# A planner that knows traced durations and the SBUF ports that VectorE and GpSimd share, in an attention-and-FFN kernel on one core

## Chip, core and metric

The kernel runs on one core of a Trainium2 chip. The metric is device time in microseconds: before, 1008.44 us is the median of three runs (1007.25 to 1010.76). One execution was profiled: its own time is 1007.83 us, and its span, from the first to the last instruction, is 1005.8 us. Engines carry the names of the profile: PE is TensorE (PEld its weight loads), DVE is VectorE, ACT is ScalarE, POOL is GpSimd, SP is SyncE, which issues the DMAs.

## The reference

Thresholded attention for 8 batches, 8 heads, 576 positions and head dimension 64, then a gated FFN over all heads side by side (512 columns), all in float32:

```python
scores = q @ k.T / sqrt(64)
scores = where(scores >= max(scores) - tau, scores, -1e9)
attn = exp(scores - max(scores))
attn = attn / (sum(attn) + 1e-9)
x = attn @ v                                  # heads side by side: 8 x 576 x 512
x_prev = x shifted by one position, zero first
xk = mu_k * x + (1 - mu_k) * x_prev
xr = mu_r * x + (1 - mu_r) * x_prev
out = sigmoid(xr @ w_r) * (relu(xk @ w_k) ** 2 @ w_v)
```

## The kernel before

**Attention.** The work is cut into 32 jobs (8 batches by 4 pairs of heads). `operands` loads q and k of a job (`rq`, `rk`) and splits them into high and low parts for TensorE (`qa`, `qb`, `kc`): copies on ACT (L480, L498), one subtraction on POOL (L488), one on DVE (L508). A job has five units: four blocks of 128 queries for both heads, and "T", the last 64 queries of both heads together. For a unit `scores` runs the matmuls (L578, for T L562) into PSUM tiles `s` (three buffers, which the outputs of attention use too). `softmax` then takes for each of the nine score tiles of a job the negated row maximum on DVE (L624), adds the threshold to it (L632), runs a steep Prelu and an Exp with row sum on ACT (L640, L648); `invert` adds 1e-9 to the row sums and takes the reciprocal on DVE (L656, L657), for both heads of a unit in one instruction each; POOL scales the rows (L671); `turn` transposes 32x32 blocks on DVE (L688, L692). `attend` multiplies by v on PE (L717), and ACT puts the result into `xT` (L743; two buffers, one per batch in flight) and `xE` (L750). The row statistics of a unit lie in a tile `sm` of 128 x 4 x 2: the statistic first, then the head.

**Weights.** w_k, w_r and w_v come in as 64-bit words in 20 pieces of 512 KB. `weight` rebuilds each piece and splits it: ACT L397, DVE L405, L419, L426, L436, ACT L443, POOL L447, in four scratch columns inside `xT[1]`.

**FFN.** 18 chunks of 256 positions: two "main" ones per batch and one "end" chunk for the last 64 positions of four batches. `ffn_chunk` mixes x and its shifted copy (POOL L816, DVE L825), splits the mix (ACT L838, POOL L846), multiplies by w_k (PE L868), squares and splits (ACT L876 to L881, POOL L891), multiplies by w_r (L910) and w_v (L932), applies the sigmoid (ACT L918) and the gate (DVE L938).

**Order.** No engine's order is written by hand. Each step is added to a `Plan` with its engine, `occ` (how long it holds the engine), `lat` (when its result is there; `occ + 0.1` if not given), a key, and the tiles it reads and writes. `Plan.order` is a list scheduler: it goes through time with its own model of the engines, at each turn takes for each engine the step that could start first (ties by key) and of these the earliest one. The key is the place in the program plus a number for the step's kind (`NUDGE`; `FIRST` for the first 60 keys); `AHEAD` moves attention's PE steps ahead of the FFN's, `LATE` adds to their dependences after time `FROM`. W0 to W3 are the times from which the planner lets the loads of the 20 pieces start. What comes out is only the order of each engine's instructions; on the chip they run when what they wait for is there.

```python
                    t = max(t, f)
                    late = t + s.soft
                    ...
                    k = (late, s.key, i, t)
                    if pick is None or k < pick:
                        pick = k
                if pick is not None and (best is None or pick[0] < best[0]):
                    best = (pick[0], e, pick[2], pick[3])
```

Of the kernel before, what the change touches and what calls it, by code (L numbers as in the profile page):

```python
# [7 lines left out]
F32 = mybir.dt.float32  # L8
FR = mybir.dt.float32r
AF = mybir.ActivationFunctionType  # L10
ALU = mybir.AluOpType
# [38 lines left out]
class Plan:  # L50
# [3 lines left out]
    HOP, LATE, FROM, AHEAD = 0.05, 0.05, 200.0, 65.0  # L54
    SOFT = {"DVE": 0, "ACT": 0}
    NUDGE = {
# [7 lines left out]
    }  # L64
    FIRST, UNTIL = {
# [8 lines left out]
    CHUNK, FETCH = 256, 3.55  # L74
# [62 lines left out]
    def order(self, loose=()):  # L137
# [904 lines left out]
```

## Time and profile before

| | |
|---|---|
| median of three runs | 1008.44 us |
| profiled execution, its own time | 1007.83 us |
| its span | 1005.8 us |
| PE busy | 900.2 us, 90% of the span |
| ACT busy | 794.9 us, 79% |
| DVE busy | 705.8 us, 70% |
| POOL busy | 588.6 us, 59% |
| mean granted TensorE clock | 0.948 of full |

Busy shares are means over stages that differ, so the span is read in stages below. A matmul's time in the profile overlaps that of the next one; what a piece of PE work really takes is read from the distance between starts. An idle engine costs time only where its work is what ends last.

### The profile page before, as it was taken

Reading aid. Unit: us, or ns where it says so; the run is one execution under the profiler, and the core shown is the slowest. Engines: PE = TensorE matmul, PEld = TensorE weight load, DVE = VectorE, ACT = ScalarE, POOL = GpSimd, SP = SyncE. Lnnn points to the kernel's source line nnn. Section 1 sums busy time; section 2 is a strip of 40 time slices with the busy share of each in tenths; the row PEclk is TensorE's granted clock in tenths of the full one; section 3 lists DMA queues with packets and bytes.
Section 4 is the critical chain, followed back from the end, with each engine's and each line's share of the span. In section 5 each row is a group of like instructions: output and inputs, shape, how many; then the busy total and the mean of one; then the engine's idle time right before and its main releaser. Section 6 shows DMA issues by size and latency. Waiting matters only on the chain.

```text
span 1005.8 us, 32052 instructions
## 1 busy us (share of the span) xinstructions
PE 900.2 (90%) x13520; PEld 790.3 (79%) x13520; DVE 705.8 (70%) x1434; ACT 794.9 (79%) x1660; POOL 588.6 (59%) x576
## 2 busy tenths in 40 slices
PE   3355669899989999999999999999999999999988
PEld 3244558798878988898889798888888888889876
DVE  5979999677878686868686958686858677741130
ACT  5766878788889898989898798888898979854422
POOL 1756667665656665756565657565666657543431
PEclk9577778899999999999999999999999999999999
DMA  7562231233323232333222223332322222210001
GB/s 282 179 252 82 89 105 50 72 117 103 110 96 117 96 117 96 117 97 103 98 99 91 77 76 117 96 117 84 118 72 89 94 90 73 70 49 22 22 22 22
DMA packets 31599, 97.48 MB, mean 97 GB/s; under 512 B 3808, under 2 KB 3808, under 8 KB 27360
## 3 DMA queue, kind: packets, MB, share of 16 engines
q1 hardware_dynamic: 31456, 95.44, 28.1%
q8 instruction: 106, 1.74, 0.7%
q14 instruction: 37, 0.30, 0.1%
HBM read 85.99 MB, written 9.44 MB: 95 GB/s over the span
## 4 chain that ended last, share of the span: by engine, by line
PE 43%; DVE 9%; ACT 4%; POOL 3%; issue 2%; ACTq 0%; DVEq 0%; POOLq 0%
PE w L868 13%; PE s L717 8%; PE w L932 7%; PE w L910 7%; PE s L578 6%; DVE r L825 3%; DVE sm L624 2%; DVE sq L688 2%; PE s L562 2%; POOL sq L671 1%; POOL xk L846 1%; ACT sq L640 1%; ACT sq L648 1%; ACT L648 1%; DVE sm L656 1%
## 5 line engine op out<-in xcount | busy, mean ns | idle before, releaser
L671 POOL TENSOR_SCALAR sq<-sq,sm 128x576 f32<-128x576 f32 x288 | 239.4, 843 | 162.4 <-DVE sm L657 90.6
L624 DVE TENSOR_REDUCE sm<-s 128x1 f32<-128x576 f32 x288 | 211.9, 745 | 81.6 <-PE s L578 75.7
L640 ACT ACTIVATE sq<-s,sm 128x576 f32<-128x576 f32 x288 | 206.4, 737 | 59.2 <-DVE sm L632 55.5
L868 PE MATMUL w<-xk,wk 128*128 128x256 f32 x1728 | 228.8, 285 | 4.0 <-ACT xk L838 2.3
L868 PEld LDWEIGHTS w<-xk,wk 128*128 128x128 f32 x1728 | 217.7, 191 | 9.6 <-issue 4.2
L648 ACT ACTIVATE sq<-sq,small 128x576 f32<-128x576 f32 x288 | 222.9, 777 | 2.0
L932 PE MATMUL w<-wv,k 128*128 128x512 f32 x864 | 215.2, 394 | 0.0
L688 DVE STREAM_TRANSPOSE sq<-sq 128x1152 f32<-128x1152 f32 x128 | 175.5, 1371 | 54.8 <-POOL sq L671 54.5
L717 PE MATMUL s<-sq,v 32*64 32x144 f32 x9216 | 177.8, 292 | 19.2 <-issue 8.4
L717 PEld LDWEIGHTS s<-sq,v 32*64 32x64 f32 x9216 | 151.0, 133 | 44.2 <-issue 23.8
L932 PEld LDWEIGHTS w<-wv,k 128*128 128x128 f32 x864 | 157.8, 188 | 32.5 <-issue 3.6
L578 PE MATMUL s<-kc,qa 128*128 128x288 f32 x512 | 128.4, 334 | 50.3 <-ACT sq L640 37.6
L578 PEld LDWEIGHTS s<-kc,qa 128*128 128x128 f32 x512 | 88.7, 204 | 78.0 <-ACT sq L640 35.2
L488 POOL TENSOR_TENSOR kc<-rk,kc 64x576 fp32r<-64x576 f32 x64 | 96.8, 1517 | 82.0 <-issue 60.8
L846 POOL TENSOR_TENSOR xk<-r,xk 128x512 fp32r<-128x512 f32 x72 | 95.3, 1324 | 83.8 <-ACT xk L838 82.8
L578 PE MATMUL s<-kc,qb 128*128 128x288 f32 x512 | 117.7, 314 | 0.0
L891 POOL TENSOR_TENSOR k<-r,k 128x512 fp32r<-128x512 f32 x72 | 93.2, 1298 | 40.1 <-ACT k L881 38.1
L910 PE MATMUL w<-wr,xk 128*128 128x512 f32 x432 | 107.1, 393 | 0.0
L825 DVE SCALAR_TENSOR_TENSOR r<-r,mu_sb,xT 128x256 f32<-128x256 f32 x128 | 73.9, 618 | 37.9 <-POOL xk L846 22.3
L578 PEld LDWEIGHTS s<-kc,qb 128*128 128x128 f32 x512 | 89.5, 205 | 1.2 <-issue 1.2
L910 PEld LDWEIGHTS w<-wr,xk 128*128 128x128 f32 x432 | 78.9, 189 | 14.5 <-ACT r L876 0.3
L838 ACT ACTIVATE xk<-r 128x512 fp32r<-128x512 f32 x72 | 45.2, 628 | 54.6 <-DVE r L825 54.3
(53 smaller groups left out, 915.2 us busy)
## 6 DMA issues: line engine op xcount, KB each, us to landing
v<-in_v SPq DMA_DIRECT2D x32, 1152.0 KB, 5.1
rq<-in_qk SPq DMA_DIRECT2D x64, 288.0 KB, 2.9
rk<-in_qk SPq DMA_DIRECT2D x64, 288.0 KB, 2.9
out<-sg SPq DMA_DIRECT2D x32, 256.0 KB, 2.1
wk<-in_w_k SPq DMA_DIRECT2D x8, 512.0 KB, 7.9
wv<-in_w_v SPq DMA_DIRECT2D x8, 512.0 KB, 10.5
wr<-in_w_r SPq DMA_DIRECT2D x4, 512.0 KB, 6.5
out<-sg SPq DMA_DIRECT2D x8, 128.0 KB, 2.4
```

Source lines behind the costliest of these rows:

```text
L578: PE.matmul(ss[y].get()[:, z, 0:HS], l.get()[:, c * P : (c + 1) * P], r.get()[:, keys(z)], start=(j == 0), stop=(j == 1),)
L624: lambda sv=sv, col=col: V.tensor_reduce(col(0), sv(), axis=AX.XY, op=ALU.max, negate=True),
L640: lambda st=st, pv=pv, col=col: A.activation(pv(), st(), AF.Prelu, bias=col(1), alpha=STEEP),
L648: lambda y=y, col=col: A.activation(part(y), part(y), AF.Exp, bias=small.get()[:, 3:4], accum_out=col(2)),
L671: lambda y=y: G.tensor_scalar(part(y), part(y), sm.get()[:, 3, y : y + 1], 0.0, op0=ALU.mult, op1=ALU.add),
L688: V.transpose(t, t)
L717: PE.matmul(os[a // 2].get()[hs, a % 2, 0:NX], vt.get()[rows, j, hs], sq.get()[rows, j, h], start=(j == 0), stop=(j == NB - 1),)
L825: V.scalar_tensor_tensor(d.get()[:, y, o : o + n], diff.get()[:, y, o : o + n], mu_sb.get()[:, j, hc + y : hc + y + 1], prv[:, hc + y], op ...
L846: lambda j=j, d=d, cs=cs: G.tensor_tensor(mix[j].get()[:, 1, cs], d.get(), mix[j].get()[:, 0, cs].bitcast(F32), op=ALU.subtract),
L868: PE.matmul(h.get()[:, f], l, r, start=(ct == 0 and i == 0), stop=(ct == NCT - 1 and i == 2))
L910: PE.matmul(z.get(), l, r, start=(ct == 0 and i == 0), stop=(ct == NCT - 1 and i == 2))
L932: PE.matmul(vps.get(), l, r, start=(ft == 0 and i == 0), stop=(ft == NFT - 1 and i == 2))
```

## The change

The planner is told other numbers and one more rule; the arithmetic of the kernel stays. First, `occ` and `lat` of most steps are set to durations from a trace. Second, steps on POOL and the DVE kinds in `PORT` (the four weight steps L405 to L436, L508 and L825) exclude each other in the planner's time: none of the one side starts before the last one of the other has ended. Third, the keys, `AHEAD`, `LATE` and the times of the weight loads have other values. Fourth, the tile `sm` is now 128 x 2 x 4, so that the two heads' sums of a unit lie four columns apart instead of side by side. Lines of the changed kernel stand 7 lower than before (L578 is now L585, L868 now L875).

```diff
-    HOP, LATE, FROM, AHEAD = 0.05, 0.05, 200.0, 65.0
+    HOP, LATE, FROM, AHEAD = 0.05, 0.3, 200.0, 120.0
     NUDGE = {
-        "act1": -59.5, "act10": 67.0, "act11": -222.0, "act12": -115.0, "act13": 59.5, "act14": -52.5, "act15": 165.0,
+        "act1": -99.5, "act10": 60.5, "act11": -242.0, "act12": -214.0, "act13": 90.5, "act14": -122.0, "act15": 167.5,
...
+    PORT = {"dve5", "dve6", "dve7", "dve8", "dve7b", "dve14"}
...
+        port = {}
...
                     t = max(t, f)
+                    if e == "POOL" or s.kind in self.PORT:
+                        t = max(t, port.get("DVE" if e == "POOL" else "POOL", 0.0))
                     late = t + s.soft
...
             s.start = t
+            if e == "POOL" or s.kind in self.PORT:
+                port[e] = t + s.occ
...
-    W0, W1, W2, W3, AVK = 3.220, 2.801, 34.671, 0.000, 1.0
+    W0, W1, W2, W3, AVK = 2.696, 1.270, 14.345, 0.000, 1.0
...
             "DVE",
-            0.65,
+            0.6,
             lambda: V.scalar_tensor_tensor(
                 u(), word(0), 29, u(), op0=ALU.logical_shift_right, op1=ALU.bitwise_or
             ),
             reads=[words],
             writes=box,
-            key=key, kind="dve8",
+            key=key, lat=0.68, kind="dve8",
...
-        sm = unit["sm"] = sbuf("sm", [P, 4, 2], F32, 4)
+        sm = unit["sm"] = sbuf("sm", [P, 2, 4], F32, 4)
...
-                return sm.get()[:, j, y : y + 1]
+                return sm.get()[:, y, j : j + 1]
...
-            V.tensor_scalar(sm.get()[:, 2, ysl], sm.get()[:, 2, ysl], 1e-9, None, op0=ALU.add)
-            V.reciprocal(sm.get()[:, 3, ysl], sm.get()[:, 2, ysl])
+            V.tensor_scalar(sm.get()[:, ysl, 2], sm.get()[:, ysl, 2], 1e-9, None, op0=ALU.add)
+            V.reciprocal(sm.get()[:, ysl, 3], sm.get()[:, ysl, 2])
```

What moves is seen at three places. The first is SP's queue from the start of the program: v and the first pieces of the weights, then q and k of jobs 1 and 2. Before, the queue stands so from its 14th DMA on:

```order
L471 DMA rk_136<-in_qk 128x576
L388 DMA wk_0_145<-in_w_k 128x512
L388 DMA wk_0_173<-in_w_k 128x512
L388 DMA wk_0_196<-in_w_k 128x512
L463 DMA rq_219<-in_qk 128x576
L388 DMA wk_0_224<-in_w_k 128x512
L463 DMA rq_229<-in_qk 128x576
L388 DMA wk_0_243<-in_w_k 128x512
L471 DMA rk_250<-in_qk 128x576
L471 DMA rk_287<-in_qk 128x576
L463 DMA rq_323<-in_qk 128x576
L388 DMA wr_0_331<-in_w_r 128x512
```

Now from its 14th:

```order
L478 DMA rk_123<-in_qk 128x576
L470 DMA rq_131<-in_qk 128x576
L395 DMA wk_0_140<-in_w_k 128x512
L470 DMA rq_145<-in_qk 128x576
L395 DMA wk_0_147<-in_w_k 128x512
L395 DMA wk_0_157<-in_w_k 128x512
L395 DMA wr_0_187<-in_w_r 128x512
L395 DMA wr_0_192<-in_w_r 128x512
L395 DMA wr_0_202<-in_w_r 128x512
L395 DMA wr_0_207<-in_w_r 128x512
L395 DMA wv_0_214<-in_w_v 128x512
L395 DMA wv_0_221<-in_w_v 128x512
```

All 20 pieces now stand ahead of the first load for job 2; before, the four loads of q and k for job 2 and one for job 3 stood ahead of the last twelve pieces.

The second place is DVE up to the first transpose of job 0 (L688 and L692, now L695 and L699). Before:

```order
L405 TENSOR_SCALAR xT_72<-xT_72 128x512
L632 TENSOR_SCALAR sm_177<-sm_177,small 128x1
L419 TENSOR_SCALAR xT_72<-xT_72 128x512
L656 TENSOR_SCALAR sm_147<-sm_147 128x1
L657 RECIPROCAL sm_147<-sm_147 128x1
L624 TENSOR_REDUCE sm_177<-s_183 128x1
L426 SCALAR_TENSOR_TENSOR xT_72<-wk_0_86,xT_72 128x512
L632 TENSOR_SCALAR sm_177<-sm_177,small 128x1
L692 STREAM_TRANSPOSE sq_149<-sq_149 128x36x16
```

Now:

```order
L433 SCALAR_TENSOR_TENSOR xT_72<-wk_0_116,xT_72 128x512
L412 TENSOR_SCALAR xT_72<-xT_72 128x512
L443 SCALAR_TENSOR_TENSOR xT_72<-wk_0_116,xT_72 128x512
L515 SCALAR_TENSOR_TENSOR qb_305<-rq_145,small,qa_301 128x576
L426 TENSOR_SCALAR xT_72<-xT_72 128x512
L433 SCALAR_TENSOR_TENSOR xT_72<-wk_0_140,xT_72 128x512
L443 SCALAR_TENSOR_TENSOR xT_72<-wk_0_140,xT_72 128x512
L412 TENSOR_SCALAR xT_72<-xT_72 128x512
L426 TENSOR_SCALAR xT_72<-xT_72 128x512
L695 STREAM_TRANSPOSE sq_152<-sq_152 128x36x32
```

Before, the first piece was still unfinished at that transpose; now six are finished there.

The third place is PE around the first matmul of the FFN (L868, now L875), with score matmuls (L578, now L585) and the T units (L562, now L569) beside it. Before:

```order
L578 MATMUL s_1632<-kc_1290,qb_1294 128x288 x2
L868 MATMUL w_1649<-xk_1120,wk_0_246 128x256 x3
L868 MATMUL w_1649<-xk_1120,wk_0_281 128x256 x3
L578 MATMUL s_1662<-kc_1585,qa_1575 128x288 x2
L578 MATMUL s_1662<-kc_1585,qb_1589 128x288 x2
L578 MATMUL s_1670<-kc_1290,qa_1280 128x288 x2
L578 MATMUL s_1670<-kc_1290,qb_1294 128x288 x2
L868 MATMUL w_1649<-xk_1120,wk_0_298 128x256 x3
```

Now:

```order
L585 MATMUL s_1661<-kc_1297,qa_1289 128x288 x2
L585 MATMUL s_1661<-kc_1297,qb_1337 128x288 x2
L569 MATMUL s_1678<-kc_1297,bd 128x288 x4
L569 MATMUL s_1678<-kc_1579,bd 128x288 x4
L875 MATMUL w_1694<-xk_1213,wk_0_209 128x256 x3
L875 MATMUL w_1694<-xk_1213,wk_0_256 128x256 x3
L585 MATMUL s_1707<-kc_1579,qa_1576 128x288 x2
L585 MATMUL s_1707<-kc_1579,qb_1636 128x288 x2
```

The T unit of the sixth job has moved ahead of the first FFN matmul; before it came 16 rows behind it. On PE the last 75 rows are the same in both, save for line numbers.

## Rows read from the trace of the kernel before

**Rows 1.** The page: span, engines, and 40 slices of 25.1 us.

```profile
span 1005.8 us, 32052 instructions
...
PE 900.2 (90%) x13520; PEld 790.3 (79%) x13520; DVE 705.8 (70%) x1434; ACT 794.9 (79%) x1660; POOL 588.6 (59%) x576
...
PEclk9577778899999999999999999999999999999999
```

**Rows 2.** Windows: start:end, length, busy us (instructions) by engine, PE clock, DMA.

```profile
0.00:12.50 12.50, 2.25 (x9) 2.25 (x10) 2.56 (x8) 4.69 (x9) 2.98 (x6) 1.00 0.78 280
12.50:152.60 140.10, 74.99 (x1357) 62.25 (x1356) 130.95 (x244) 105.67 (x227) 80.42 (x74) 0.71 0.43 153
152.60:210.00 57.40, 53.83 (x812) 47.32 (x812) 45.46 (x92) 46.16 (x99) 39.42 (x36) 0.91 0.22 78
210.00:905.20 695.20, 677.14 (x10815) 597.02 (x10813) 509.13 (x1040) 602.35 (x1270) 431.36 (x428) 1.00 0.29 95
905.20:1005.80 100.60, 92.04 (x539) 81.44 (x531) 17.66 (x52) 36.06 (x59) 34.43 (x34) 0.97 0.07 22
```

**Rows 3.** Waits on PE, 210 to 910 us: total, times, longest.

```profile
PE s L578 <- ACT sq L640: 5.1, 9, 0.9
PE s L717 <- ACT sq L640: 4.5, 4, 2.2
```

**Rows 4.** Groups of DVE instructions by form, 12.5 to 152.6 us: busy, mean ns.

```profile
L624 DVE TENSOR_REDUCE sm<-s 128x1 f32<-128x576 f32 x47 | 34.5, 744 | 10.9 <-PE s L578 10.0 <-PE s L562 0.9
...
L405 DVE TENSOR_SCALAR xT<-xT 128x512 f32<-128x512 f32 x17 | 11.9, 720 | 0.0
L508 DVE SCALAR_TENSOR_TENSOR qb<-rq,small,qa 128x576 fp32r<-128x576 f32 x11 | 11.7, 1073 | 0.0
L419 DVE TENSOR_SCALAR xT<-xT 128x512 uint32<-128x512 uint32 x17 | 10.7, 644 | 0.0
...
L825 DVE SCALAR_TENSOR_TENSOR r<-r,mu_sb,xT 128x256 f32<-128x256 f32 x6 | 5.7, 984 | 0.0
L656 DVE TENSOR_SCALAR sm<-sm 128x2 f32<-128x2 f32 x18 | 4.8, 269 | 0.2 <-ACT sq L648 0.2
...
L656 DVE TENSOR_SCALAR sm<-sm 128x1 f32<-128x1 f32 x5 | 0.7, 143 | 0.0
```

**Rows 5.** Single lines, whole span: count, shortest/median/longest in ns.

```profile
L405 DVE TENSOR_SCALAR xT<-xT x20: 402/419/1644, 18.5 to 175.9; 128x512 f32<-128x512 f32 x20
...
L419 DVE TENSOR_SCALAR xT<-xT x20: 409/423/1493, 18.9 to 177.3; 128x512 uint32<-128x512 uint32 x20
...
L508 DVE SCALAR_TENSOR_TENSOR qb<-rq,small,qa x64: 770/810/2035, 6.9 to 861.7; 128x576 fp32r<-128x576 f32 x64
...
L825 DVE SCALAR_TENSOR_TENSOR r<-r,mu_sb,xT x128: 443/479/1660, 94.6 to 941.4; 128x256 f32<-128x256 f32 x128
```

**Rows 6.** Timeline of DVE, then of POOL, from 618 us: start, length.

```profile
618.81 1.26 DVE L656 TENSOR_SCALAR sm<-sm 128x2 f32<-128x2 f32 x1
...
618.14 1.91 POOL L846 TENSOR_TENSOR xk<-r,xk 128x512 fp32r<-128x512 f32 x1
```

**Rows 7.** Timeline of PE, DVE and SP's queue in the first stage.

```profile
59.98 0.46 PE L717 MATMUL s<-sq,v 32*64 32x144 f32 x4 [3.93 <-issue]
...
61.21 0.76 DVE L624 TENSOR_REDUCE sm<-s 128x1 f32<-128x576 f32 x1 [4.97 <-PE s L578]
...
43.90 7.64 SPq L388 DMA_DIRECT2D wv<-in_w_v  x8
```

**Rows 8.** Timeline of PE late in the long stretch.

```profile
863.99 0.42 PE L578 MATMUL s<-kc,qa 128*128 128x288 f32 x2
...
865.05 1.55 PE L932 MATMUL w<-wv,k 128*128 128x512 f32 x6
...
875.99 0.53 PE L578 MATMUL s<-kc,qa 128*128 128x288 f32 x2
876.36 0.43 PE L578 MATMUL s<-kc,qb 128*128 128x288 f32 x2
```

More of the change, by code (lines that the diff above doesn't have):

```diff
@@ L399, in weight @@
             writes=box,
-            key=key, kind="act1",
+            key=key, lat=0.67, kind="act1",
         )
@@ L403, in weight @@
             "DVE",
-            0.4,
+            0.333,
             lambda: V.tensor_scalar(t(), t(), W_MIN, W_MAX, op0=ALU.max, op1=ALU.min),
             writes=box,
-            key=key, kind="dve5",
+            key=key, lat=0.42, kind="dve5",
         )
@@ L430, in weight @@
             writes=box,
-            key=key, kind="dve7",
+            key=key, lat=0.69, kind="dve7",
         )
@@ L440, in weight @@
             writes=box,
-            key=key, kind="dve8",
+            key=key, lat=0.68, kind="dve8",
         )
-        add("ACT", 0.53, lambda: A.activation(piece.get()[:, 0], t(), AF.Copy), reads=box, writes=[(piece, 0)], key=key, kind="act2")
+        add("ACT", 0.52, lambda: A.activation(piece.get()[:, 0], t(), AF.Copy), reads=box, writes=[(piece, 0)], key=key, lat=0.63, kind="act2")
         add(
             "POOL",
-            1.27,
+            1.24,
             lambda: G.tensor_tensor(piece.get()[:, 1], t(), piece.get()[:, 0].bitcast(F32), op=ALU.subtract),
@@ L449, in weight @@
             writes=[(piece, 1)],
-            key=key, kind="pool1",
+            key=key, lat=1.28, kind="pool1",
         )
@@ L482, in operands @@
                 writes=[both],
-                key=key - PREP, kind="act4",
+                key=key - PREP, lat=0.68, kind="act4",
             )
@@ L492, in operands @@
                 writes=[both],
-                key=key - PREP, kind="pool2",
+                key=key - PREP, lat=1.44, kind="pool2",
             )
@@ L502, in operands @@
                 writes=[top],
-                key=key - PREP, kind="act3",
+                key=key - PREP, lat=0.78, kind="act3",
             )
@@ L517, in operands @@
                 writes=[low],
-                key=key - PREP, kind="dve7b",
+                key=key - PREP, lat=0.81, kind="dve7b",
             )
@@ L553, in scores @@
                         writes=[(bd, (v_, h))],
-                        key=key - 3, kind="act5",
+                        key=key - 3, lat=0.25, kind="act5",
                     )
@@ L626, in softmax @@
                 writes=[(sm, (0, y))],
-                key=key - KMAX, kind="dve9",
+                key=key - KMAX, lat=0.75, kind="dve9",
             )
@@ L634, in softmax @@
                 writes=[(sm, (1, y))],
-                key=key - KMAX, kind="dve10",
+                key=key - KMAX, lat=0.2, kind="dve10",
             )
@@ L642, in softmax @@
                 writes=[p[y]],
-                key=key - KEXP, kind="act6",
+                key=key - KEXP, lat=0.74, kind="act6",
             )
@@ L650, in softmax @@
                 writes=[p[y], (sm, (2, y))],
-                key=key - KMASK, kind="act7",
+                key=key - KMASK, lat=0.95, kind="act7",
             )
@@ L664, in softmax @@
             writes=[(sm, (3, y)) for y in ys],
-            key=n + 0.5, kind="dve11",
+            key=n + 0.5, lat=0.38, kind="dve11",
         )
@@ L669, in softmax @@
                 "POOL",
-                0.715,
+                0.72,
                 lambda y=y: G.tensor_scalar(
-                    part(y), part(y), sm.get()[:, 3, y : y + 1], 0.0, op0=ALU.mult, op1=ALU.add
+                    part(y), part(y), sm.get()[:, y, 3:4], 0.0, op0=ALU.mult, op1=ALU.add
                 ),
@@ L675, in softmax @@
                 writes=[p[y]],
-                key=n - 1.0, kind="pool3",
+                key=n - 1.0, lat=0.76, kind="pool3",
             )
@@ L694, in turn @@
         if unit["kind"] == "P":
-            add("DVE", 1.27, main, writes=[(sq, (c, 0)), (sq, (c, 1))], key=n - 1.0, kind="dve12")
+            add("DVE", 1.292, main, writes=[(sq, (c, 0)), (sq, (c, 1))], key=n - 1.0, lat=1.38, kind="dve12")
         else:
-            add("DVE", 0.7, tail, writes=[(sq, (c, 1))], key=n - 1.0, kind="dve13")
+            add("DVE", 0.69, tail, writes=[(sq, (c, 1))], key=n - 1.0, lat=0.77, kind="dve13")
     def attend(job, key):
@@ L754, in put_tail @@
                 )
-            add("ACT", 0.3, put, reads=[os[a]], writes=main, key=key - 5, kind="act8")
-            add("ACT", 0.1, put_tail, reads=[os[a]], writes=tail, key=key - 5, kind="act9")
+            add("ACT", 0.265, put, reads=[os[a]], writes=main, key=key - 5, lat=0.39, kind="act8")
+            add("ACT", 0.077, put_tail, reads=[os[a]], writes=tail, key=key - 5, lat=0.2, kind="act9")
     def edge(b, key):
@@ L840, in ffn_chunk @@
                     writes=[(mix[j], (0, hc))],
-                    key=key, kind="act10",
+                    key=key, lat=0.63, kind="act10",
                 )
@@ L850, in ffn_chunk @@
                     writes=[(mix[j], (1, hc))],
-                    key=key, kind="pool6",
+                    key=key, lat=1.3, kind="pool6",
                 )
@@ L875, in ffn_chunk @@
             r = sbuf("r", [P, 512], F32, 2)
[L876 to L877 removed]
+            add("ACT", 0.478, lambda r=r, h=h: A.activation(r.get(), h.get().rearrange("p a b -> p (a b)"), AF.Relu), reads=[h], writes=[r], key=key - 20, lat=0.6, kind="act11")
+            add("ACT", 0.52, lambda r=r: A.activation(r.get(), r.get(), AF.Square), writes=[r], key=key - 1, lat=0.63, kind="act12")
             add(
                 "ACT",
[L880 removed]
+                0.52,
                 lambda r=r, js=js: A.activation(
@@ L885, in ffn_chunk @@
                 writes=[(k2, (0, j))],
-                key=key - 1, kind="act13",
+                key=key - 1, lat=0.63, kind="act13",
             )
@@ L895, in ffn_chunk @@
                 writes=[(k2, (1, j))],
-                key=key - 1, kind="pool7",
+                key=key - 1, lat=1.3, kind="pool7",
             )
@@ L940, in ffn_chunk @@
                 writes=[(sg, j)],
-                key=key - 20, kind="dve15",
+                key=key - 20, lat=0.68, kind="dve15",
             )
```

35 lines of the change are left out of this document (16 added, 19 removed), and 27 rows, old and new, of the table NUDGE.

## The prediction

> **What bounds the kernel now.** Read the engines' shares first: PE is busy for 90% of the span [rows 1]. That is a mean over unlike stages, so the windows come next [rows 2]. Up to 152.6 us, where the first matmul of the FFN starts, PE has only attention: in the 140.1 us from 12.5 on it is busy for 74.99 at a granted clock of 0.71, while DVE is busy for 130.95 (93%). That stage is DVE's: it does the row maxima and transposes of five jobs and at the same time most of the weight pieces. From 152.6 to 905.2 us PE is busy for 53.83 + 677.14 of 752.6 us, so it is the bound, with 3.6 + 18.1 = 21.7 us idle; ACT, the next, is at 602.35 of 695.20 (87%). The last 100.6 us are the FFN of the last chunks alone. PE's order there is the same before and now, so nothing changes in it.
>
> So the change can act in three places: on when the FFN can start, on how much work is left then, and on the 21.7 us.
>
> **Part one: DVE and POOL get in each other's way.** Look at one step of DVE, the addition of 1e-9 to two sums [rows 6]: it starts at 618.81 and takes 1.26 us, ending at 620.07, while a POOL step runs from 618.14 to 620.05. It ended when POOL did. The same step on one column takes 0.143 us [rows 4]. The Trainium skill has this as a rule ("SBUF — State Buffer", section "Who interferes with whom"): GpSimd and some VectorE steps share one port pair, whoever starts first keeps it for the whole instruction, and the other blocks. By that rule the trace agrees.
>
> What it costs in DVE's stage is read as mean there [rows 4] less median over the whole span [rows 5], times the count: L405 17 x (0.720 - 0.419) = 5.1 us; L419 17 x (0.644 - 0.423) = 3.8; L508 11 x (1.073 - 0.810) = 2.9; L825 6 x (0.984 - 0.479) = 3.0; and the two-column sums, against their one-column form, 18 x (0.269 - 0.143) = 2.3. Together 17.1 us of a stage in which DVE is the bound. The planner now knows of this. But it sets an order, no times: on the chip nothing holds a step back until the other engine is done, and a plan that is off by a microsecond puts steps of 0.4 to 1.3 us side by side again. What it can do is prefer steps that never block (row maxima, transposes) while POOL is busy, and POOL is busy for 80.42 of the 140.1 us [rows 2]. Ends: 0 and -17.1 us. I take -5, between a quarter and a third: order survives a shift, turns don't.
>
> In this, the sums four columns apart are worth 0 to -2.3 us. I take 0: the only form that is seen not to block has one element, and the new one still has two. A rule of the Trainium skill says the same: "VectorE: DVE Perf Modes", section "Mode 2×_2P — use both read ports for one tensor", lets a step with one source use both ports whenever source and destination lie in SBUF and the outermost dimension of more than one element is even, whatever the step between elements. By it the new layout saves nothing; without it -2.3. No run here has shown it yet.
>
> **Part two: loads of the weights.** Before, SP's queue issued the eight pieces of w_v from 43.90 us on, for 7.64 us, because loads for jobs 2 and 3 stood ahead of them and waited for their buffers. At 56 to 60 us PE stood 3.93 us for "issue" in the first products with v, and DVE then 4.97 us for its scores [rows 7], nearly half of the 10.9 us that it waited for PE in this stage [rows 4]. Now all twenty pieces stand ahead of the loads for job 2, and six of them are finished on DVE by the first transpose, where before it was none. Whether the wait for "issue" came from these loads the trace does not say; but DVE has then less left to fit in later, and the loads are done earlier. Ends: 0 and -5.0. I take -3.
>
> **Part three: work ahead of the first FFN matmul.** The mix that this matmul waits for needs the third pair of L825. Counted in DVE's order, what stands ahead of it changes little: 46 row maxima for 45 (0.744 us each), one L419 more (0.423), one L508 less (0.810), and four shorter steps more (an L426, two L632, one inversion), which I put at 0.35 each: 0.744 + 0.423 - 0.810 + 1.4 = +1.8 us.
>
> On PE more attention is done by then: 180 of the first kind of score matmul for 172 (L578), and six T units for five (8 matmuls of L562). Eight L578 take from 863.99 to 865.05, 1.06 us [rows 8]. Eight of L562 have the same width, so I take the same: -2.1 us of what is left for the stage in which PE is the bound. Ends 0 and -2.1.
>
> **Part four: the long stretch.** PE's order changes 452 times between attention and FFN, for 426 before. A change costs PE something: two score matmuls after another kind take 0.37 us to the next start (875.99 to 876.36), and four without one 0.53 us, or 0.26 for two [rows 8]. Up to 0.1 us each: 0 to +2.6, I take 0.05: +1.3. Against that, attention is now further ahead: at the w_k matmuls of the fifth chunk 14 jobs' worth of scores are issued for 13.25, and 13 jobs are multiplied by v for 12. So the waits for ACT's Prelu, 5.1 + 4.5 us in this stretch [rows 3], have more lead. Of the 21.7 us idle I take -3. Ends: -9.6, those waits whole, and the loss of rival B.
>
> **Sum**, against the profiled execution's own 1007.83 us: -5 (blocked steps) -3 (loads) +1.8 (DVE steps ahead) -2.1 (attention done) +1.3 (changes on PE) -3 (waits) = -10.0, so 997.8. The median of the runs shown, 1008.44, is 0.6 above that execution; with it the forecast is **998.4 us**.
>
> **Rivals.**
> *A: the start gains nothing.* The port rule is a lock and not a share, so planned turns may only move the block from one engine to the other; and if the wait for "issue" belongs to PE's instructions and not to the loads, it stays. Then -5 and -3 fall away: 1006.4, within 0.3% (3 us, about what a measurement of this kernel can tell from no change) of before. For it: the lock is real, and DVE's order ahead of the FFN is as long as before. Against it: 17.1 us is a lot to leave untouched.
> *B: slower, by ACT in the long stretch.* ACT is at 87% there and takes its steps in order. A softmax issued earlier pushes back the copies that free PSUM for PE, and `s` has three buffers for scores and outputs together. PE's waits on L640 there average (5.1 + 4.5) / (9 + 4) = 0.74 us [rows 3]. One more such wait for each of the 27 jobs after the first five is +20 us in place of -3: 1021.4. It decides from 7.0 / 27 = 0.26 us a job on, where the rest of the gain is eaten. For it: 87% leaves little. Against it: PE idles for only 18.1 us in that stretch now, so ACT has kept up with an order with less lead.
> *C: the turns work in full.* -17.1 in place of -5: 986.3. For it: the planner no longer fills POOL's time with steps that can't run. Against it: the drift above.
>
> **Chances.** Forecast 0.50, A 0.17, B 0.23, C 0.10. A and the forecast's edge lie astride the border: of A 0.02 falls on either side. So faster by over 0.3%: 0.50 + 0.10 + 0.02 = 0.62; within: 0.13; slower: 0.23 + 0.02 = 0.25. The likely case has its own range: blocked steps 0 to -10, loads 0 to -5, waits 0 to -6 about the rest, 1.0: 988 to 1009. The range for 8 in 10 reaches down past C by the part of the waits that I left out, to 984, and up to where the lighter half of B lies, 1016.
>
> **What would show it.** In the changed profile the first w_k matmul should start at about 146.4 us (152.6 less 5 and 3, plus 1.8), L405 and L419 should have means below 0.6 us, and the wait of DVE for PE up to there should be under 8 us. If the two-column sums still have single steps over 1 us, the layout did nothing. From that matmul to the start of the tail 752.6 - 2.1 + 1.3 - 3 = 749 us should pass. If the start of the FFN does not move and this stretch shrinks, the gain is not where I put it; if the stretch grows and PE's waits on L640 there exceed 20 us in all, it was B. The prediction is wrong if the start comes later than 152.6 us, or if PE idles for over 30 us in the stretch.

## Result, and the profile after

The changed kernel takes **994.03 us** (median of four runs, 992.16 to 995.05); the kernel before, on the same chip, 1009.15 us. The ratio is 0.9849, with a 95% interval of 0.9825 to 0.9872: 15.1 us less. The profiled execution of the changed kernel has an own time of 993.96 us and a span of 992.1 us; the numbers below are from it.

First the page of the changed kernel, the lines that answer to [rows 1]:

```profile
span 992.1 us, 32003 instructions
...
PE 896.4 (90%) x13520; PEld 785.9 (79%) x13520; DVE 700.8 (71%) x1434; ACT 797.4 (80%) x1660; POOL 576.3 (58%) x576
...
PEclk9577787999999999999999999999999999999999
```

Every engine has as many instructions in these counts as before, and PE has the same work. Its shares hardly move. So the windows of the changed kernel have to say where 13.7 us of the span went. Columns as in [rows 2]; the cuts lie at the same events: 157.6 us is the first matmul with w_k (L875), 890.7 us the last product with v.

```profile
0.00:12.50 12.50, 3.22 (x12) 2.90 (x12) 4.57 (x12) 6.07 (x11) 2.97 (x6) 1.00 0.77 270
12.50:157.60 145.10, 78.66 (x1368) 65.87 (x1369) 133.67 (x258) 112.79 (x244) 83.83 (x79) 0.69 0.43 152
157.60:215.00 57.40, 55.52 (x1059) 48.65 (x1065) 50.94 (x96) 50.32 (x104) 39.76 (x39) 0.98 0.29 92
215.00:890.70 675.70, 666.10 (x10567) 586.33 (x10550) 494.04 (x1017) 592.05 (x1244) 415.32 (x420) 1.00 0.30 96
890.70:992.10 101.40, 92.90 (x541) 82.12 (x534) 17.56 (x52) 36.14 (x59) 34.44 (x34) 0.97 0.07 21
```

Set beside [rows 2]:

| stage | before | after | difference |
|---|---|---|---|
| up to the first w_k matmul | 152.6 | 157.6 | +5.0 |
| from there to the last product with v | 752.6 | 733.1 | -19.5 |
| tail | 100.6 | 101.4 | +0.8 |

The start comes later. All of the gain, and more, lies in the stage in which PE is the bound. There PE's idle time falls from 21.6 to 11.5 us (57.40 - 55.52 and 675.70 - 666.10), which is 10.1 of the 19.5, and its busy time from 730.97 to 721.62 us, which is 9.4. Of these 9.4, some 2.1 is attention that PE now does before the start (the prediction's count), and some 0.7 is left to the tail, which opens with 30 of L939's matmuls for 27. The rest goes roughly with the granted clock. Over the first 57.4 us of the stage it is 0.98 where it was 0.91, by an estimate worth 0.07 x 57.4 = 4.0 us. From 250 to 300 and from 800 to 850 us it is 1.00 where it was 0.97, by the same estimate 3.0 us together. The windows of the kernel before:

```profile
250.00:300.00 50.00, 46.04 (x760) 40.46 (x751) 36.51 (x74) 45.11 (x97) 31.21 (x32) 0.97 0.32 107
800.00:850.00 50.00, 47.81 (x630) 42.90 (x616) 37.66 (x78) 41.48 (x94) 30.77 (x31) 0.97 0.28 95
```

The clock's two levels are 1.2 and 2.4 GHz, so 1.00 is the upper one throughout. Before, the loss in the first stretch follows a gap on PE, seen in the kernel before's timeline of PE (start, length, in brackets the idle time ahead and what ended it) and in its windows cut at that gap:

```profile
184.61 2.29 PE L562 MATMUL s<-kc,bd 128*128 128x288 f32 x8 [2.94 <-ACT sq L640]
186.70 0.68 PE L578 MATMUL s<-kc,qa 128*128 128x288 f32 x2
```

```profile
152.60:184.60 32.00, 28.44 (x434) 25.50 (x433) 28.36 (x53) 27.05 (x62) 25.89 (x22) 0.93 0.23 78
184.60:200.00 15.40, 15.39 (x239) 13.17 (x240) 9.65 (x21) 12.24 (x24) 10.02 (x10) 0.80 0.09 33
```

Two L578 matmuls take 0.68 us here for 0.42 in [rows 8], and the clock of the stretch behind the gap is 0.80. The windows of the changed kernel, cut at the same distance from its first w_k matmul, show 0.96 and 1.00: there is no such gap.

```profile
157.60:189.60 32.00, 31.33 (x629) 28.16 (x629) 28.45 (x51) 27.20 (x58) 21.10 (x22) 0.96 0.25 77
189.60:205.00 15.40, 15.40 (x170) 13.27 (x169) 14.14 (x31) 13.70 (x34) 11.45 (x11) 1.00 0.47 154
```

So this wait cost more than its length: 2.94 us itself, and by an estimate another 0.20 x 15.4 = 3.1 us in matmuls at the lower level behind it. Cut finer, the clock is 1.00 from 178.0 to 181.0 us, 0.50 from 184.6 to 190.0 and 1.00 again from 193.0 us on. The two later windows of 0.97 hold one gap of 2.2 us each. What [rows 3] counted has become smaller in the changed kernel (its waits on PE, 215 to 891 us: total, times, longest):

```profile
PE s L585 <- ACT sq L647: 2.1, 4, 0.8
PE s L724 <- ACT sq L647: 1.9, 2, 1.7
```

Together 4.0 us for 9.6 before.

**Why the start is later.** The mix of the first chunk is not what holds it. In the changed kernel's timeline of DVE and ACT the third pair of L832 starts at 146.26 us (before, L825 at 147.84 us), and ACT's copy of the mix follows at 148.27 us (before 151.32 us). Then PE, in its own timeline:

```profile
146.26 1.78 DVE L832 SCALAR_TENSOR_TENSOR r<-r,mu_sb,xT 128x256 f32<-128x256 f32 x2
...
148.27 0.62 ACT L845 ACTIVATE xk<-r 128x512 fp32r<-128x512 f32 x1
```

```profile
152.90 0.85 PE L585 MATMUL s<-kc,qa 128*128 128x288 f32 x2 [1.59 <-ACT sq L647]
153.54 0.68 PE L585 MATMUL s<-kc,qb 128*128 128x288 f32 x2
155.55 2.29 PE L569 MATMUL s<-kc,bd 128*128 128x288 f32 x8 [1.32 <-ACT sq L647]
157.63 1.48 PE L875 MATMUL w<-xk,wk 128*128 128x256 f32 x6
```

PE's order now puts more scores, the T unit of the sixth job among them, ahead of the first w_k matmul, and each of these waits until a Prelu on ACT has freed a buffer of `s`. The two Prelus concerned wait in their turn for DVE, for the threshold of their rows (the changed kernel's timelines of ACT and DVE):

```profile
152.10 0.74 ACT L647 ACTIVATE sq<-s,sm 128x576 f32<-128x576 f32 x1 [1.69 <-DVE sm L639]
...
154.75 0.74 ACT L647 ACTIVATE sq<-s,sm 128x576 f32<-128x576 f32 x1 [1.00 <-DVE sm L639]
```

```profile
151.81 0.20 DVE L639 TENSOR_SCALAR sm<-sm,small 128x1 f32<-128x1 f32 x1
...
154.52 0.20 DVE L639 TENSOR_SCALAR sm<-sm,small 128x1 f32<-128x1 f32 x1
```

So DVE still has a part in when the FFN starts, by its thresholds and not by the mix. The copy of the mix is done at 148.89 us; POOL's part, which the later matmuls of the group need, runs from 153.54 to 154.80 us. The first w_k matmul comes 2.8 us after that, behind the T unit. Part of this delay is not lost: the T unit is work that PE need not do later.

**DVE in that stage.** The groups of DVE that answer to [rows 4], same columns, 12.5 to 157.6 us of the changed kernel:

```profile
L631 DVE TENSOR_REDUCE sm<-s 128x1 f32<-128x576 f32 x47 | 34.6, 747 | 8.9 <-PE s L585 5.7 <-PE s L569 3.0
L515 DVE SCALAR_TENSOR_TENSOR qb<-rq,small,qa 128x576 fp32r<-128x576 f32 x11 | 10.9, 1001 | 0.0
L426 DVE TENSOR_SCALAR xT<-xT 128x512 uint32<-128x512 uint32 x17 | 9.8, 589 | 0.1
L412 DVE TENSOR_SCALAR xT<-xT 128x512 f32<-128x512 f32 x17 | 9.8, 590 | 0.4 <-ACT xT L404 0.3
...
L663 DVE TENSOR_SCALAR sm<-sm 128x2 f32<-128x2 f32 x21 | 5.9, 281 | 0.2
...
L832 DVE SCALAR_TENSOR_TENSOR r<-r,mu_sb,xT 128x256 f32<-128x256 f32 x8 | 4.4, 590 | 0.0
...
L663 DVE TENSOR_SCALAR sm<-sm 128x1 f32<-128x1 f32 x5 | 0.7, 145 | 0.1
```

By the working of the prediction's part one, the time above the median is 17 x (0.590 - 0.419) = 2.9 us for L412, 17 x (0.589 - 0.423) = 2.8 for L426, 11 x (1.001 - 0.810) = 2.1 for L515, 8 x (0.590 - 0.479) = 0.9 for L832 and 21 x (0.281 - 0.145) = 2.9 for the two-column sums: 11.6 us for 17.1. These five kinds are less blocked, by about the forecast amount. The prediction's count leaves out the two other weight steps in `PORT`, L426 and L436 (now L433 and L443). Their mean in this stage rose from 0.790 us (32 steps) to 0.843 us (33 steps), 1.8 us more in all. And DVE's busy time in the stage did not fall (133.67 us for 130.95), because it does more steps there (258 for 244).

Over the whole span the two-column sums got longer, 42.6 us for 34.2 before, and the one-column form is what it was (the changed kernel's groups of DVE by form):

```profile
L663 DVE TENSOR_SCALAR sm<-sm 128x2 f32<-128x2 f32 x128 | 42.6, 333 | 51.6 <-ACT sq L655 51.4
L663 DVE TENSOR_SCALAR sm<-sm 128x1 f32<-128x1 f32 x32 | 4.5, 141 | 2.3 <-ACT sq L655 2.1
```

One of them, in the changed kernel's timeline of POOL and DVE:

```profile
349.14 3.05 POOL L495 TENSOR_TENSOR kc<-rk,kc 64x576 fp32r<-64x576 f32 x2 [2.03 <-issue]
...
350.87 1.35 DVE L663 TENSOR_SCALAR sm<-sm 128x2 f32<-128x2 f32 x1
352.25 0.17 DVE L664 RECIPROCAL sm<-sm 128x2 f32<-128x2 f32 x1
352.33 0.19 DVE L639 TENSOR_SCALAR sm<-sm,small 128x1 f32<-128x1 f32 x1
```

It takes 1.35 us and ends at 352.22, when POOL's steps do (352.19), as in [rows 6]. Behind it stands L639, a row's threshold, for which ACT's Prelu waits. This addition is not among the kinds in `PORT`, so the planner does nothing to keep it away from POOL's steps.

### The profile page after: what moved, and what is told of

The parts are those of the page before. It is cut to its first block, busy times and chain, and to the rows that moved or that the text cites. A ratio compares the mean times of both kernels' runs of the same rounds, so it can differ in the third digit from the quotient of the medians.

```text
span 992.1 us, 32003 instructions
## 1 busy us (share of the span) xinstructions
PE 896.4 (90%) x13520; PEld 785.9 (79%) x13520; DVE 700.8 (71%) x1434; ACT 797.4 (80%) x1660; POOL 576.3 (58%) x576
## 4 chain that ended last, share of the span: by engine, by line
PE 65%; DVE 16%; ACT 10%; issue 4%; POOL 2%; DMA 2%; SPq 0%; ACTq 0%; POOLq 0%; DVEq 0%
PE w L875 16%; PE s L724 15%; PE w L939 14%; PE s L585 10%; PE w L917 8%; DVE sm L631 4%; ACT sq L647 3%; DVE sq L695 3%; ACT sq L655 3%; PE s L569 3%; DVE r L832 2%; DVE sm L663 1%; DVE qb L515 1%; POOL sq L678 1%; DMA wk<-in_w_k 1%
## 5 line engine op out<-in xcount | busy, mean ns | idle before, releaser
L678 POOL TENSOR_SCALAR sq<-sq,sm 128x576 f32<-128x576 f32 x288 | 233.0, 821 | 166.9 <-DVE sm L664 90.6
L875 PE MATMUL w<-xk,wk 128*128 128x256 f32 x1728 | 227.9, 284 | 4.7 <-ACT xk L845 2.3
L875 PEld LDWEIGHTS w<-xk,wk 128*128 128x128 f32 x1728 | 217.1, 190 | 9.1 <-issue 3.0
L939 PE MATMUL w<-wv,k 128*128 128x512 f32 x864 | 215.6, 394 | 0.0
L695 DVE STREAM_TRANSPOSE sq<-sq 128x1152 f32<-128x1152 f32 x128 | 175.3, 1371 | 40.8 <-POOL sq L678 40.4
L724 PE MATMUL s<-sq,v 32*64 32x144 f32 x9216 | 179.8, 294 | 13.1 <-ACT sq L647 5.0
L939 PEld LDWEIGHTS w<-wv,k 128*128 128x128 f32 x864 | 157.0, 188 | 32.3 <-issue 4.0
L585 PE MATMUL s<-kc,qa 128*128 128x288 f32 x512 | 124.2, 326 | 63.1 <-ACT sq L647 41.3
L585 PEld LDWEIGHTS s<-kc,qa 128*128 128x128 f32 x512 | 87.6, 200 | 88.1 <-ACT sq L647 43.7
L585 PE MATMUL s<-kc,qb 128*128 128x288 f32 x512 | 115.2, 309 | 3.1 <-DVE qb L515 3.1
L495 POOL TENSOR_TENSOR kc<-rk,kc 64x576 fp32r<-64x576 f32 x64 | 92.8, 1461 | 40.7 <-issue 17.7
L832 DVE SCALAR_TENSOR_TENSOR r<-r,mu_sb,xT 128x256 f32<-128x256 f32 x128 | 65.3, 552 | 37.0 <-POOL xk L853 21.8
L585 PEld LDWEIGHTS s<-kc,qb 128*128 128x128 f32 x512 | 87.2, 200 | 4.6 <-DVE qb L515 3.8
L663 DVE TENSOR_SCALAR sm<-sm 128x2 f32<-128x2 f32 (+1 forms) x160 | 47.1, 294 | 53.9 <-ACT sq L655 53.5
```

Source lines behind the costliest of these rows:

```text
L585: PE.matmul(ss[y].get()[:, z, 0:HS], l.get()[:, c * P : (c + 1) * P], r.get()[:, keys(z)], start=(j == 0), stop=(j == 1),)
L678: lambda y=y: G.tensor_scalar(part(y), part(y), sm.get()[:, y, 3:4], 0.0, op0=ALU.mult, op1=ALU.add),
L695: V.transpose(t, t)
L724: PE.matmul(os[a // 2].get()[hs, a % 2, 0:NX], vt.get()[rows, j, hs], sq.get()[rows, j, h], start=(j == 0), stop=(j == NB - 1),)
L875: PE.matmul(h.get()[:, f], l, r, start=(ct == 0 and i == 0), stop=(ct == NCT - 1 and i == 2))
L939: PE.matmul(vps.get(), l, r, start=(ft == 0 and i == 0), stop=(ft == NFT - 1 and i == 2))
```

## Experiments

All runs have the kernel before beside them on the same chip (medians of 1009.1 us or within 0.2 us of it). The theory after the result had four candidates for the 15 us: the layout of `sm`, the rule on ports, the lead (`AHEAD`, `LATE`), and the order as a whole. The long stretch in the table and below is all of it, from the first w_k matmul to the last product with v.

| kernel | median us (runs) | ratio to before [95%] | first w_k matmul, us | PE idle in the long stretch, us |
|---|---|---|---|---|
| before | 1009.15 (4) | 1 | 152.6 | 21.6 |
| after | 994.03 (4) | 0.9849 [0.9825, 0.9872] | 157.6 | 11.5 |
| e1_layout | 1009.25 (10) | 1.0004 [0.9990, 1.0018] | 153.7 | 21.9 |
| e2_keys | 1031.10 (4) | 1.0226 [1.0200, 1.0252] | 158.3 | 34.7 |
| e3_durations | 1036.80 (4) | 1.0284 [1.0260, 1.0308] | 181.2 | 22.2 |
| e4_no_port | 1025.45 (4) | 1.0173 [1.0150, 1.0195] | 160.2 | 31.0 |
| e5_old_lead | 1007.88 (10) | 0.9987 [0.9971, 1.0003] | 154.8 | 21.6 |
| e6_hop_after | 1020.74 (4) | 1.0115 [1.0093, 1.0138] | 164.9 | 26.0 |
| e7_hop_before | 1032.42 (4) | 1.0237 [1.0218, 1.0256] | 159.1 | 34.1 |
| e8_no_add | 979.07 (4) | 0.9709 [0.9688, 0.9730] | 152.5 | 5.0 |
| e9_hop_no_port | 1020.19 (4) | 1.0103 [1.0088, 1.0118] | 167.7 | 20.1 |
| e12_hop_045 | 1010.53 (10) | 1.0016 [0.9999, 1.0033] | 150.5 | 24.9 |
| e10_hop_old_lead | 1016.22 (5) | 1.0067 [1.0042, 1.0092] | 152.7 | 28.1 |
| e11_before_no_add | 994.54 (4) | 0.9851 [0.9834, 0.9868] | 150.7 | 14.8 |

### The layout alone (e1_layout)

The kernel before, with the tile `sm` of after; its order of instructions is that of before.

```diff
-        sm = unit["sm"] = sbuf("sm", [P, 4, 2], F32, 4)
+        sm = unit["sm"] = sbuf("sm", [P, 2, 4], F32, 4)
...
-            V.tensor_scalar(sm.get()[:, 2, ysl], sm.get()[:, 2, ysl], 1e-9, None, op0=ALU.add)
+            V.tensor_scalar(sm.get()[:, ysl, 2], sm.get()[:, ysl, 2], 1e-9, None, op0=ALU.add)
```

> The kernel before with the sums of a unit four columns apart and nothing else; no engine's order moves. Theory 'no port is freed': the two-column addition stays at a mean of 0.25 to 0.35 us with single steps over 1 us, and the time stays within 3 us of before. Rival 'the layout frees the port': its mean falls to about 0.15 us, DVE's busy time by about 15 us, and the time by 0 to 4 us.

Measured: 1009.25 us, ratio 1.0004 [0.9990, 1.0018]. Its group of two-column sums, over the whole span:

```profile
L656 DVE TENSOR_SCALAR sm<-sm 128x2 f32<-128x2 f32 x128 | 34.4, 269 | 32.8 <-ACT sq L648 32.3
```

The kernel before has 128 of them with a mean of 267 ns and a longest of 1.267 us; here the longest is 1.275 us. The layout alone changes neither the step nor the time by anything that these runs can tell. By the Trainium skill, "VectorE: DVE Perf Modes", section "Mode 2×_2P — use both read ports for one tensor", a one-source step between SBUF places can use both ports if its outermost dimension of more than one element is even; the section sets no condition on the distance between elements. By that rule this run agrees, at a distance of four (269 ns for 267).

### One half of the change each (e2_keys, e3_durations)

e2 has the numbers of after (keys, `AHEAD`, `LATE`, load times) in the planner of before, with its old durations and no rule on ports. e3 is the counterpart: the planner of after with the numbers of before. The first cut shows what e2 lacks against after (not shown: the other durations and the old layout of `sm`), the second e3 against after:

```diff
-                    if e == "POOL" or s.kind in self.PORT:
-                        t = max(t, port.get("DVE" if e == "POOL" else "POOL", 0.0))
...
-            0.558,
+            0.56,
...
-            key=key, lat=0.67, kind="act1",
+            key=key, kind="act1",
```

> The kernel before with the keys, the lead of attention and the load times of the changed one, but with the old durations in the planner and without the port rule. Theory 'the lead makes the gain': 994 to 1001 us, PE idle under 15 us from the first w_k matmul to the last product with v. Rival 'keys and planner fit only together': above 1005 us, PE idle there over 20 us.

```diff
-    HOP, LATE, FROM, AHEAD = 0.05, 0.3, 200.0, 120.0
+    HOP, LATE, FROM, AHEAD = 0.05, 0.05, 200.0, 65.0
...
-        "act1": -99.5, "act10": 60.5, "act11": -242.0, "act12": -214.0, "act13": 90.5, "act14": -122.0, "act15": 167.5,
+        "act1": -59.5, "act10": 67.0, "act11": -222.0, "act12": -115.0, "act13": 59.5, "act14": -52.5, "act15": 165.0,
...
-    W0, W1, W2, W3, AVK = 2.696, 1.270, 14.345, 0.000, 1.0
+    W0, W1, W2, W3, AVK = 3.220, 2.801, 34.671, 0.000, 1.0
```

> The changed kernel (traced durations, port rule, new layout) with the keys, the lead and the load times of before. Theory 'the lead makes the gain': 1004 to 1014 us, PE idle in the long stretch near the 21.7 us of before. Rival 'a planner that knows more makes the gain': 994 to 1001 us, with PE idle there near the 11.5 us of the changed kernel.

Measured: 1031.10 and 1036.80 us, both slower than before, by 2.3% and 2.8%. For e2 the rival was right (above 1005 us, PE idle over 20 us); for e3 neither expectation was. They lose at different places. Their longest waits on PE over the whole span, first of e2, then of e3:

```profile
PE s L580 <- POOL kc L490: 37.2, 3, 16.4
```

```profile
PE s L568 <- ACT sq L646: 37.3, 2, 37.1
```

In e2 the first of the three waits for a job's `kc` from POOL is the 8.6 us at the start of the program; the other two, 28.5 us (before 3.2 us, one time), lie ahead of the first w_k matmul, which comes only 5.7 us later than before. Most of e2's loss is in the long stretch, 773 us for 753. In e3 a single wait of 37.1 us stands in the first stage, and the first w_k matmul is at 181.2 us; its long stretch is shorter than before, 746 us. So neither half can be said to be worth a part of the 15 us: in these runs the numbers and the planner only serve together. That alone doesn't show that the new durations or the rule are better; numbers that were found for one planner may simply not fit another. That is tested next.

### A neutral disturbance of the planner (e6_hop_after, e7_hop_before, e12_hop_045)

`HOP` is the planner's delay from one engine to the next. It is 0.05 us in both kernels; here it is 5 ns more, or 5 ns less. The rule, the durations and the keys stay.

```diff
-    HOP, LATE, FROM, AHEAD = 0.05, 0.3, 200.0, 120.0
+    HOP, LATE, FROM, AHEAD = 0.055, 0.3, 200.0, 120.0
```

> The changed kernel with its planner's constant for the way between two engines at 0.055 us in place of 0.050, which says nothing of ports, lead or durations. Theory 'the order fits its planner': the order found by the keys is lost, 1005 to 1035 us, as much as the port rule's removal cost (1025 us). Rival 'the port rule is what counts': 992 to 1000 us, since the rule is still there.

> The kernel before with the same constant at 0.055 us. Theory 'the order fits its planner': slower than before by 5 to 35 us, as its keys too were fitted to a planner. Rival: within 5 us of before.

> The changed kernel with the constant at 0.045 us. Theory 'the order fits its planner': slower than 994 by 10 to 35 us, as at 0.055 us. Rival 'the changed planner's orders are good in general, 0.055 was bad luck': 990 to 1000 us.

Measured: after goes from 994.03 to 1020.74 us (+26.7) and 1010.53 us (+16.5); before goes from 1009 to 1032.42 us (+23.4). A number that says next to nothing about the chip costs more than the whole change gains. All three came out as 'the order fits its planner' had it. The largest row of waits on PE in e6, over the whole span (the changed kernel has 41.3 us there in 21):

```profile
PE s L585 <- ACT sq L647: 60.2, 26, 11.6
```

Of these 60.2 us 52.5 lie ahead of the first w_k matmul, which comes 7.3 us later than in after; the long stretch takes some 22 us more, with 26.0 us of idle time on PE for 11.5. So both kernels stand on an order that fits its planner closely, and in these three runs it cost 16 to 27 us to lose that fit. An experiment that changes the planner and loses this much has shown that loss and nothing more.

### The rule on ports (e4_no_port, e9_hop_no_port)

e4 is after without the rule. e9 is the same with `HOP` at 0.055, so that both it and e6 are off their fit, and only the rule differs between them.

```diff
-                    if e == "POOL" or s.kind in self.PORT:
+                    if False:
...
-            if e == "POOL" or s.kind in self.PORT:
+            if False:
```

> The changed kernel, its planner without the rule that POOL and the port kinds of DVE exclude each other; all else is kept. Theory 'the lead makes the gain': 993 to 1000 us, blocked steps on DVE as in the changed kernel. Rival 'the turns make the gain': above 1003 us, and the first weight steps (0.564 and 0.618 us in the changed kernel) back at means above 0.65 us.

> The changed kernel with the constant at 0.055 us and without the port rule, to be set beside the one with the rule at 0.055 us (1020.74 us). There neither order is the one that the keys were fitted to. Theory 'the rule itself is worth little': 1012 to 1030 us, no clear order of the two. Rival 'the rule is worth a lot': 1035 us or more, with means of the first weight steps above 0.65 us.

Measured: e4 takes 1025.45 us, 31.4 above after. Taken by itself that reads like a large worth of the rule, but it is near the size of the neutral disturbance (16.5 and 26.7). The largest of its new waits on PE (over the whole span, e4):

```profile
PE s L585 <- POOL kc L495: 17.2, 3, 15.0
PE s L724 <- ACT bd L553: 13.7, 2, 7.6
PE s L585 <- POOL sq L678: 11.1, 1, 11.1
```

The 15.0, the 13.7 and the 11.1 us all lie ahead of the first w_k matmul, which comes only 2.6 us later than in after; most of the loss is in the long stretch, 764 us for 733.

The pair without a fit answers better: 1020.74 us with the rule, 1020.19 without it. So no run shows that the rule is worth time in itself. One such pair can't exclude a worth of some us either, as the order alone moves the time by more.

What the rule does to the steps is seen. All steps of the kinds in `PORT`, 336 in each kernel, take 206.8 us together in after and 219.7 in e4, 211.8 in e6 and 217.9 in e9 (count times mean, added up over DVE's groups by form; before 221.2). So with the rule these steps are blocked for 6 to 13 us less. The means of the first weight steps, L412 and L426, came out on either side of 0.65 us without the rule: 0.513 and 0.721 us in e4, 0.502 and 0.731 in e9. What remains possible, and was not tried, is that a planner with the rule lets a search find better keys; for that the keys would have to be found anew with and without it.

### The lead (e5_old_lead, e10_hop_old_lead)

After, with `AHEAD` and `LATE` of before; e10 is the same on e12.

```diff
-    HOP, LATE, FROM, AHEAD = 0.05, 0.3, 200.0, 120.0
+    HOP, LATE, FROM, AHEAD = 0.05, 0.05, 200.0, 65.0
```

> The changed kernel with the old lead of attention (AHEAD 65, LATE 0.05); planner and keys are kept. Theory 'the order fits its planner, and any part replaced breaks it': 1010 to 1040 us, with two or more single waits on PE of over 5 us after the first stage or a longer first stage. Rival 'the lead alone makes the gain': 1004 to 1012 us, with many short waits of PE for the Prelu and no long one.

> The changed kernel with the constant at 0.045 us and the old lead (AHEAD 65, LATE 0.05), to be set beside the one at 0.045 us. Theory 'the lead spares PE waits in the long stretch': slower than that one, PE idle in the long stretch higher by 5 us or more. Rival 'the lead is only a part of the fit': no slower than that one by more than 5 us, PE idle there alike.

Measured: e5 takes 1007.88 us: of the 15.1 us 13.9 are gone, and PE's idle time in the long stretch is 21.6 us, as before the change. Its windows (columns as in the rows of before; the start is at 154.8 us, the tail from 890 us):

```profile
154.80:890.00 735.20, 713.56 (x11547) 628.71 (x11549) 540.61 (x1110) 634.93 (x1339) 448.16 (x453) 0.99 0.29 95
890.00:1003.70 113.70, 104.39 (x612) 91.58 (x594) 19.33 (x56) 42.60 (x68) 39.21 (x38) 0.98 0.06 19
```

Less of the FFN is done beside attention, so the tail is 12.3 us longer (113.70 for 101.40), and PE waits more. The time lies in the rival's range, but not by many waits for the Prelu: in the two rows that [rows 3] counted e5 has 7.7 us in 8 waits, after 4.0, and PE's waits for "issue" ahead of products with v rise more, from 1.2 to 9.0 us. So the forecast mechanism of part four, a lead that spares waits for the Prelu, is the smaller part, and the control weakens it further: with `HOP` at 0.045 the same edit costs 5.7 us (1010.53 to 1016.22), and PE's idle time rises only from 24.9 to 28.1 us, so that neither expectation for e10 is met in full. Both pairs point the same way, and both are smaller than what 5 ns of `HOP` do. How much of the gain is the lead's is left open.

### Without the blocked step (e8_no_add, e11_before_no_add)

The blocked sums of the profile are the addition of 1e-9. The row's largest score contributes exp(0) = 1 to the sum, so the sum is about 1 or more, and in float32 the addition changes nothing. Both kernels without it:

```diff
-            V.tensor_scalar(sm.get()[:, ysl, 2], sm.get()[:, ysl, 2], 1e-9, None, op0=ALU.add)
```

> The changed kernel without the addition of 1e-9 to the sums, which is left out; the reciprocal takes the sums themselves. No engine's order moves otherwise. It takes away 42.6 + 4.5 us of DVE work, 20 of them blocked. Theory 'DVE is the bound only up to the first w_k matmul': 26 additions of 0.15 to 0.28 us fall away there, so the first w_k matmul comes 3 to 7 us earlier, and the time falls by 2 to 6 us, to 988 to 992. Rival 'PE's order sets the start': the time stays within 1.5 us of 994.

> The kernel before without the addition of 1e-9 to the sums, which is left out; its order is kept. Theory 'the blocked step costs where DVE is on the path': 996 to 1004 us, the first w_k matmul 3 to 6 us earlier than 152.6 and PE idle in the long stretch below 21.7 us. Rival 'only the changed order can use DVE's time': within 4 us of 1009.

Measured: **979.07 us** on after (-15.0) and 994.54 us on before (-14.5), more than either theory expected (2 to 6 and 5 to 13 us). The planner sees the same steps, keys and durations in each pair, so the orders differ by the missing instruction alone. Neither loses a fit, which is why this pair can be read. The second one takes as much from the kernel before as the whole change did, and the first is the fastest kernel of this study: 3% below before.

The windows of e8 (first w_k matmul 152.5 us, tail from 874.1 us):

```profile
12.50:152.50 140.00, 79.83 (x1369) 67.60 (x1370) 124.59 (x230) 111.69 (x243) 86.82 (x80) 0.68 0.44 157
152.50:209.90 57.40, 55.58 (x1083) 49.30 (x1088) 49.01 (x85) 50.13 (x104) 39.53 (x38) 0.97 0.28 93
209.90:874.10 664.20, 661.07 (x10542) 585.34 (x10526) 464.30 (x894) 589.23 (x1244) 415.47 (x420) 1.00 0.30 97
```

Only 5.1 us of the gain come from the start, where DVE is the bound (in the kernel before 1.9 us). The long stretch is shorter by 733.1 - 721.6 = 11.5 us, PE idles for 5.0 us there instead of 11.5, and yet DVE is busy for only 73% of its larger part in after (494.04 of 675.70 us). One path is seen in the records of ACT's Prelu: how long ACT stood before it until a threshold came, over the whole span, first in after, then in e8 (total, times):

```profile
  DVE sm L639: 43.9, 57
```

```profile
  DVE sm L639: 34.8, 41
```

In the kernel before it is 55.5 us, 45 times, and without the addition 42.0 us, 39 times. The addition holds DVE for up to 1.45 us while POOL has a long step; the row maxima and thresholds (L639) of the next unit stand behind it in DVE's order; the Prelu waits for the threshold; and PE waits for the buffer of `s` that the Prelu frees. At the end of this path, PE's waits for the Prelu in the long stretch fall from 4.7 to 0.5 us, 4.2 of the 6.5 us of idle time gained there. The other 5.0 of the 11.5 us are busy time of PE, of which some 2.4 went to the stages before and behind. The reciprocal, which has the same two elements, is not blocked: it takes a mean of 156 ns, and at the longest 171 ns, as the first step of `invert` (e8):

```profile
L663 DVE RECIPROCAL sm<-sm 128x2 f32<-128x2 f32 x128 | 19.9, 156 | 54.7 <-ACT sq L655 54.2
```

What these two runs don't separate is the blocking from the addition itself. Of the 42.6 us that the 128 two-column additions take in after, 128 x 0.141 = 18.0 us would remain at the mean of the one-column form, and 24.6 lie above it; leaving the addition out removes both. Two additions of one column each, which would keep the 1e-9 in the form that does not block (141 ns), would tell, but were not tried.

## Why the prediction was right in time and wrong in place

The time, 994.03 us, lies 4.4 us below the forecast of 998.4 and inside its range, and it is faster by more than 0.3%. That the sum is nearly right is luck, because large errors cancel: the start was to come 6.2 us earlier and came 5.0 later, and the stretch behind it was to be 3.8 us shorter and was 19.5 shorter.

- **Part one, blocked steps, -5 us: the size was right for the kinds counted, the effect was not.** The five kinds are blocked for 5.5 us less (17.1 to 11.6), and the weight steps that were left out of the count took 1.8 us more. L412 and L426 have means of 0.590 and 0.589 us, under the 0.6 that the prediction named. But that did not bring the start forward: what DVE saved it spent on other steps put into the stage. The step of the prediction that failed is the one that made the start of the FFN a matter of what stands ahead of the third pair of L825 in DVE's order. That pair did come 1.6 us earlier. The first w_k matmul waited for PE's own order, for scores and a T unit that waited for Prelus, and these for DVE's thresholds.
- **Layout, 0: right.** e1 shows it alone. Single steps over 1 us are still there.
- **Part two, loads, -3 us: half.** The wait of 3.93 us for "issue" in [rows 7] is gone from the first products with v, and DVE waits for PE 8.7 us in the stage (5.7 + 3.0) for 10.9; "under 8" was named. The start did not gain from it.
- **Part three, +1.8 us and -2.1 us.** The added work on PE ahead of the start was seen, but only as a gain for the later stage. That the same matmuls delay the first w_k matmul, because in this stage each waits for a Prelu to free `s`, was not counted. "The prediction is wrong if the start comes later than 152.6 us": it came at 157.6, and in this part it is wrong.
- **Part four, +1.3 us and -3 us: direction right, size off.** Waits in the long stretch fell by 10.1 us, beyond the end of -9.6 us that only the two rows of [rows 3] had given; those two fell by 5.6. Nothing was put down for the granted clock, which by the estimate above gave some 7 us more. The cost of 26 more changes on PE was not seen apart from this.
- **Rivals.** A (the start gains nothing) was right about the start and wrong about the time, since it let the long stretch gain only 3. B did not happen: the waits on the Prelu fell where it wanted them over 20 us. C is 7.7 us off in time (986.3), and its mechanism did not occur; 11.6 of its 17.1 us are still blocked.

The prediction's own sentence for this case, "if the start of the FFN does not move and this stretch shrinks, the gain is not where I put it", is what came about: the stretch took 733.1 us, where 749 was named.

What the runs put in its place: the 15 us are the gain of an order in which PE meets fewer waits once it is the bound, and runs more of that stage at the upper clock. Which of the new numbers made that order is not shown and stays open, because each part that was put back alone (the numbers, the planner, the rule, the lead) cost 13.9 to 42.8 us, and a neutral disturbance alone costs 16.5 to 26.7. The rule on ports was seen to shorten the steps that it names, but not to be worth time of its own; the layout alone was worth nothing; and the lead points the forecast way without being settled. The contention that the change plans around is real. One of its victims, left out instead of planned around, is worth 15 us in either kernel; how much of that is the blocking and how much the addition's own time is open.

## What to carry to other kernels

Before one edit to a scheduler's inputs is credited with a gain or a loss, disturb a number that should not matter and see how far the time moves; a difference below that says nothing about the edit. A step of two elements that another engine can block may stand ahead of steps that the critical engine waits for, however little of its own engine's time it takes. So look for groups whose mean is well above that of a smaller form, then for who stands behind them, and where the arithmetic allows it, try leaving the step out before planning around it. When PE is the bound, read a gap together with the granted clock behind it.

## What was not expected of the hardware

- Two elements per partition are enough to be blocked: L663 on 128x2 took up to 1.446 us while a POOL step ran, on 128x1 a mean of 0.141 us. A reciprocal of the same 128x2 kept a mean of 0.156 us, with a longest of 0.171 (e8).
- Taking out that addition, 47.1 us of DVE's busy time (42.6 + 4.5), brought 15.0 us at the end, although DVE was busy for 73% of the stretch in which most of it was gained (215 to 890.7 us); 2 to 6 us had been expected.
- Behind the gap of 2.94 us on PE that ended at 184.61 us the kernel before ran the next 15.4 us at a granted clock of 0.80, at 0.50 up to 190.0 us, without any further idle time (15.39 us busy of 15.40).
